# Hedgehog attention and squared-ReLU FFN on one core: q and k crossbar transposes in pieces of four blocks, a PSUM bank kept for zero matmuls, and a new instruction order

## The chip, the cores and the metric

One core of a Trainium2 chip runs the whole program. Times are device microseconds of an execution, given as the median of several runs. A profile is one execution with its own span, the time from the first to the last instruction that the trace holds. The engines are PE (matrix), DVE (vector), ACT (scalar), POOL and SP; SP and POOL here mainly issue DMAs.

## What is computed

```
q, k, v: [8 batches, 8 heads, 576 tokens, 64] f32;  w_phi [64, 128];  w_in [512, 2048];  w_out [2048, 512]
phi(x)  = concat(exp(p), exp(-p)),  p = x @ w_phi - max|x @ w_phi|
kv      = sum over tokens of phi(k) v^T;   z = sum over tokens of phi(k)
attn    = (phi(q) @ kv) / (phi(q) @ z + 1e-6)
x       = attn, heads side by side: [4608 tokens, 512]
out     = max(x @ w_in, 0)^2 @ w_out       [4608, 512] f32
```

Matmul operands are bf16.

## The kernel before

**Work.** Attention runs batch by batch (eight batches of 576 tokens = 512 + 64). The FFN runs in nine chunks of 512 tokens: chunk b takes the first 512 tokens of batch b, and the last chunk takes the eight remainders of 64 tokens. Attention of batch c + 1, the first FFN matmul of chunk c and the second one of chunk c - 1 are mixed, so that PE always has long FFN matmuls beside attention's short ones.

**A batch of attention.** POOL loads k, q and v and casts them to bf16 on the way (`load`, L512 and L520; `load_q`, L532). A batch's k or q lies in SBUF as 18 blocks of 128 x 128, two heads side by side: four groups of four blocks, and a "single" group of two blocks with the 64 last tokens of each head. The blocks have to be transposed. For batches 0 and 1 (`PE_IN`) PE does it (`pe_transposes`, L616), four blocks into one PSUM bank, and DVE or ACT copies them out (L439, L441). For batches 2 to 7 SP issues a crossbar DMA, one for all 18 blocks of k and one for all 18 of q (`transposed`, L626). Then, group by group:

- k: projection (PE, L670 in batch 0, L642 later), largest magnitude per token (DVE, L677, L722), two exponentials (ACT, L705, L728), the scale of v by exp of the maximum (ACT L740 and L747, then DVE L762 and L766), and the sum over tokens (PE, L783 and L788, called KV below), copied to SBUF by ACT or DVE.
- q: projection for the maximum (PE L642 or L816, DVE L823) and, transposed, for the features (PE L858, two exponentials on ACT, L873). The output of eight heads is a matmul with the positive features (PE L888, called NA), a scale of its sum in PSUM (DVE L900), a matmul with the negative ones (L888, NB), a reciprocal (DVE L908) and a product (DVE L912) into `xo`. `xo` is transposed for the FFN: in batch 0 by PE (L928) with copies by DVE (L937), later by a crossbar DMA from SP (L950, four blocks each).

Projections use 64 rows of the array, two side by side; the planner calls them "tiled". All other matmuls use 128 rows.

**FFN.** x times w_in is L1049 in chunk 0 and L1038 later; the ReLU is on ACT (L1015) or DVE (L1017), the square on DVE (L1024); times w_out is L1103 (L1067 for the last quarter); the result leaves PSUM by ACT or DVE (L441, L439) and HBM stores are issued by SP (L1121, L1118, L1090).

**What sets the order.** The program is not issued in the order of the source. Each step is an `Op` with an engine, a cost, a key and its reads and writes. `Machine.run` (a planner that runs while the program is built) replays the engines, the eight PSUM banks and two DMA queues with these costs, and at each step takes the ready Op with the smallest key. Thousands of keys (`KEYS`), release times of loads (`RELEASES`) and a string of bits (`STATES`), which says for each copy and ReLU whether ACT or DVE does it, are written out in the file; `LIM` caps how many PSUM groups of a kind may be open; `SLACK` is what the plan adds to the landing of a DMA. Each engine then issues its instructions strictly in the planned order, and a semaphore wait at the head of a queue holds all that stands behind it. POOL has at most eight DMAs under way: the ninth waits for the first.

**Zero matmuls.** After the plan is made, gaps in PE's planned time before `WARM_UP` = 45 us are filled with matmuls of a zero tile (L1195, `warm`), as many as fit into the planned gap. They write to a PSUM bank that is free at that moment (`op.spare`); where no bank is free, nothing is filled in.

Of the kernel before, what the change touches and what calls it, by code (L numbers as in the profile page):

```python
# [21 lines left out]
SLACK = {"first": 1.2, "v0": 2.5, "ld": 0.8, "x": 1.2, "kq": 1.0}  # L22
# [3 lines left out]
WARM_UP, COLD = 45.0, 6.0  # L26
# [87 lines left out]
class Machine:  # L114
# [7 lines left out]
    def __init__(self, plan, limits, ahead, patience, want):  # L122
        self.plan, self.limits = plan, limits
        self.ahead, self.patience, self.want = ahead, patience, want
        self.free_at = [0.0] * self.BANKS
        self.holding = None
        self.open = {}
        self.q = {"SP": [], "POOL": []}
        self.q_t, self.q_v = 0.0, 0
        self.hist = {"SP": [], "POOL": []}  # L130
# [64 lines left out]
    def run(self):  # L195
# [81 lines left out]
        while left:  # L277
# [19 lines left out]
            spare = next((b for b in range(self.BANKS) if self.free_at[b] <= e["free"] + 1e-9), None) if name == "PE" else None  # L297
            op = pick(name, e, t)
# [31 lines left out]
            if op.closes is not None:  # L330
                g = op.closes
# [19 lines left out]
def kernel(  # L351
# [32 lines left out]
    def pin(ins):  # L384
        i = ins.ins
        before = last_on.get(i.engine)
        if before is not None:
            dep(i, before, mybir.DependencyClass.NoSync)
        last_on[i.engine] = i.name
        if now[0].gate is not None:  # L390
            dep(i, now[0].gate.ins, mybir.DependencyClass.Sync)
        now[0].ins = i.name
        return ins
# [203 lines left out]
    def attention(b):  # L597
        s2 = b % 2
        pe_in = b in K['PE_IN']
# [24 lines left out]
        def transposed(x, xt, tag, ttag, key):  # L624
            def fn():
                pin(nc.sync.dma_start_transpose(out=xt, in_=x))  # L626
            add("SP", (2.8 if tag == "xk" else 3.4, 0), key, fn, r=of(tag, b, (0, 1, "s") if tag == "xq" else (0, 1, 2, 3, "s")),
                w=[(ttag, s2, t) for t in range(18)], dma=(3.6, HW_IN, "x", "kq"), what="X" + tag)

        if not pe_in:  # L630
            transposed(xk[s2], kTb, "xk", "kT", KA(b) - 10)
            transposed(xq[s2], qTb, "xq", "qT", KA(b) - 9)
# [345 lines left out]
        else:  # L978
            if pe_in:
# [235 lines left out]
    'PE_IN': [0, 1],  # L1215
    'PX': [1, 1, 1, 1, 1],
# [5 lines left out]
    'LIM': {'b0': 7, 'att': 3, 'kv': 7, 'op': 6},  # L1222
    'AHEAD': 356.131,
    'PATIENCE': 60.701,
# [4 lines left out]
    '1000000100001001111000110100100000000100010000001001000000010101000010000010001000010010000010000000'  # L1229
    '0100000101001010001110100010101001001000100010011001000101001001101010010100101101100010010100011100'  # L1230
    '0111010111100111100110100000111'
# [3 lines left out]
    17407, 102, 303, -19, 23448, 164, 25399, 7284, 103, -334, -342, 962, 612, -4448, -358, -466, 854, -5120, 1043,  # L1235
    1445, 2531, 2378, 1835, 1683, 1283, 2296, 2776, 6225, 1578, 6847, 9430, 23446, 3002, 6973, 2986, 4636, 7251,
    4704, 6911, 3336, 1003, 977, 1014, 1256, 2044, 19225, 3264, 1208, 2649, 9653, 3031, 2018, 7283, 1699, 1392,
    2415, 2482, 2569, 1938, 7416, 2230, 19677, 19665, 21149, 985, 631, 1829, 1167, 502, 1106, 30444, 1429, 24788,
    11688, 1068, 2741, 2271, 1691, 557, 1483, 638, 1830, 1651, 599, -401, 1899, 768, 1607, 1345, 1946, 17315, 1356,
    23984, 24358, 2102, 2748, 1812, 1047, 7206, 3044, 7208, 17205, 16309, 2884, 1937, 2580, 2117, 23465, 1319,  # L1240
    32941, 353, 6936, 22713, 1482, 1252, 12153, 9984, 23851, 1776, 1870, 28693, 2989, 3338, 9168, 2470, 2176, -1818,
    1746, -2214, 2184, 2431, 2073, 16742, 12309, 3675, 32055, 2751, 2607, 33525, 19924, 2061, 1353, 18117, 879, 666,
    2992, 2848, 2951, 3261, 32406, -843, 2706, 724, 5383, 2189, 3713, -1132, 3059, 22482, 2647, 33607, 2425, 2903,
    3153, 7467, 2946, 17043, 887, 30937, 1975, 19418, 5174, 20405, 3839, 537, 22061, 13862, 4153, 4372, 3313, 3702,
    2934, 2946, 2343, 3093, 22612, 3559, 8512, 2725, 3616, 26332, 29011, 3758, 20842, 6383, 2667, 4917, 3013, 11902,
    5345, 5238, 5921, 9912, 17625, 6541, 2315, 4379, 3435, 538, 4929, 3936, -2259, 3063, 3410, 4141, 23913, 13791,
    14506, 9834, 3978, 4002, 4288, 4215, 2945, 1909, 5362, 5104, 5553, 5287, 3268, 17046, 798, 3707, 2741, -1094,
    3553, 8533, 6784, 7264, 5884, 4403, 7199, 11290, 5958, 4782, 5787, 5872, 5644, 5916, 5299, 5137, 5079, 5080,
    20856, -473, 6391, 5749, 5537, 5046, 6063, 19035, 3357, 9582, 5994, 4922, 5968, 6119, 4977, 6670, 6244, 6483,
    6290, 6698, 19067, 4958, -996, 5517, 5252, 5391, 6788, 5266, 4299, 5039, 2805, 10740, 5284, 7476, 6917, 6887,  # L1250
    9690, 7248, 39413, 1751, 9675, 6437, 28262, 6319, 5577, 6334, 6287, 6302, 18429, 7382, 2955, 6913, 5198, 24236,
    28571, 6767, 6251, 7494, -758, 7560, 8050, 9450, 7621, 8371, 7966, 3353, 2499, 2619, 1952, 6194, 29465, 774,
    5220, 3223, 3756, 4311, 3208, 4062, 4051, 4788, 3955, 479, 4014, 3767, 3800, 3168, 4377, -1024, 4889, 5051,
    4450, 2778, 4515, 7272, 9663, 4340, 4251, 5804, 5006, 4304, 9662, 4907, 2794, 5997, 5050, 5175, 5451, 4923,
    28317, 7970, 4699, 4303, 1709, 9057, 5944, 5392, 4331, 14380, 2713, 4765, 4953, 12329, 4480, 5767, 4592, 6860,
    7810, 10905, 2818, 6137, 4180, 2215, 3286, 7321, 5283, 5241, 5956, 5275, 31537, 7305, 7279, 8169, 7954, 8774,
    7928, 7946, 7447, 7197, 8571, 8788, 8754, 9914, 9151, 8623, 10205, 28753, 9236, 8038, 8574, 22052, 8380, 8450,
    7529, 3291, -2, 11359, 9824, 9084, 13735, 9213, 10106, 8801, 8580, 8548, 9717, 12195, 21514, 9841, 10195, 9372,
    20619, 10629, 7364, 7402, 8587, 6358, 6839, 7541, 9500, 9718, 10799, 10955, 10544, 5683, 2374, 9755, 9159,
    27351, 9417, 9862, 9302, 20470, 32494, 10238, 6138, 7030, 7927, 10849, 9641, 9510, -1016, 20794, 10915, 8427,  # L1260
    -116, 13197, 9447, 9495, 2667, 692, 22484, 20389, 10746, 7094, 9290, 10721, 10810, 18159, 12068, 31380, 28083,
    22915, 1026, -887, 11060, 3635, 11045, 11396, 9857, 12004, 7583, 18462, 8756, 4983, 7513, 8752, 3219, 5133,
    6755, -1, 15253, 5347, 6465, 7754, 11386, 4931, 4785, 5572, 8512, 18443, 10833, 15727, 7521, 27495, 8162, 6150,
    7496, 8751, 8038, 7422, 7940, 3836, 10117, 6091, 22706, 7326, 7703, 13090, 9732, 23399, 8450, 13984, 975, 23532,
    8575, 9687, 9024, 7376, 8938, 10675, 9574, 7478, 8651, 8128, 8849, 5308, 31332, 21114, 8850, 29038, 9584, 6298,
    9555, 13221, 10146, 26486, 9580, 10029, 16988, 7506, 5719, 7874, 7841, 7758, 7389, 9044, 16298, 13239, 12245,
    23349, 9079, 12781, 7480, 11973, 8824, 8823, 6561, 6517, 9711, 10208, 3635, 14886, 9819, 5468, 9796, 10776,
    9740, 9730, 27385, 11031, 18006, 10703, 10132, 14, 10657, 9648, 22562, 10246, 19975, 11130, 25441, 23920, 14604,
    8983, 8228, 15704, 10056, 12998, 9196, -1267, 15126, 10713, -326, 20534, 11321, 11509, 12968, 13034, 11538,
    4820, 11603, 1244, 11706, 11438, 11864, 10659, 15019, 12774, 13092, 11103, 11910, 12865, 11965, 11827, 10973,  # L1270
    -497, 11622, 13807, 31538, 11957, 13552, 5263, 12566, 12058, 10811, 25517, 12045, 9673, -2199, 12689, 6817,
    12468, 25073, 13804, 12710, 12761, 14880, 24784, 5370, 9220, 9204, 17211, 13305, -10, 31398, 22456, 9554, 20134,
    14287, 12831, 14375, 12743, 12421, 8816, 16805, 13198, 13168, 9775, 28439, 11026, 24020, 13360, 3050, 15853,
    1925, -239, 4903, 4986, 16708, 13835, 12965, 12562, 11651, 12912, 24547, -1847, 13009, 10966, -2373, 11087,
    9756, 10945, 10200, 12118, 10502, 10956, 21707, 16803, 17099, 11772, 18442, 13381, 11449, 31507, 22778, 12610,
    11775, 11507, 4434, 11804, 11515, 11801, -528, 11413, 13866, 16900, 5711, 15578, 9473, 13709, 19170, 12569,
    10487, 13433, 22777, 22857, 1833, 12762, 24856, 12485, 11283, 14167, 10087, 13341, 8113, 15210, 20080, 16461,
    14025, 15631, 11608, 14097, 7884, 30686, 20661, 25313, -255, -2159, 24682, 11371, 10070, 11200, 16134, 3932,
# [100 lines left out]
```

## Time and profile before

| what | value |
|---|---|
| median of 8 runs | 362.9 us (361.88 to 363.99) |
| profiled execution | 362.88 us, of which the span is 360.8 us |
| PE busy | 344.7 us (96%), 3412 instructions |
| DVE busy | 292.6 us (81%), 503 instructions |
| ACT busy | 232.0 us (64%), 434 instructions |
| POOL busy | 112.6 us (31%) |
| zero matmuls (L1195) | 118 |
| first FFN matmul (L1049) | starts at 33.1 us |
| last matmul (L1067) | ends at 356.9 us |

A PE that is busy 96% of the span is not 96% useful: a matmul of 128 x 512 has a record of 379 ns, but in a long run one starts every 216 ns (40 of them take 8.63 us in the chain of work that ended last), zero matmuls count as busy, and so does a matmul at half the clock. The tables below are therefore read by starts, by stage.

### The profile page before, as it was taken

What the parts mean: (1) busy time and instruction counts of PE and PEld (TensorE: products, weight loads), DVE (VectorE), ACT (ScalarE), POOL (GpSimd) and SP (SyncE); (2) the same over time, 40 slices, a digit from 0 to 9 for tenths busy, and PEclk for the clock granted to TensorE, in tenths of its full rate; (3) what the DMA queues carried; (4) which work ended last, traced back from release to release, by engine and by line L of the source; (5) the groups of instructions that cost most, each with busy time, mean ns of one, the idle gap of its engine ahead of it and who ended that gap; (6) DMA issues with size and microseconds to landing.
All of it is one profiled execution on the core that took longest, in us unless ns stands there. A gap on an engine that the chain in (4) does not pass through costs nothing.

```text
span 360.8 us, 8564 instructions
## 1 busy us (share of the span) xinstructions
PE 344.7 (96%) x3412; PEld 198.2 (55%) x3442; DVE 292.6 (81%) x503; ACT 232.0 (64%) x434; POOL 112.6 (31%) x167
## 2 busy tenths in 40 slices
PE   8579999999999999999999999999999999999995
PEld 8378886554555555446544555555455554444444
DVE  4998999789999977899789888999798965686131
ACT  2986899588888783959677847957885340310320
POOL 8626638356635851363405211020000000000000
PEclk9959999999999999999999999999999999999999
DMA  8999999997989999898957774447230031100213
GB/s 94 192 201 140 168 187 127 168 158 101 163 146 131 157 125 182 169 149 115 89 115 93 128 94 107 96 69 122 77 100 2 17 95 45 36 0 2 110 35 89
DMA packets 102631, 39.62 MB, mean 110 GB/s; under 512 B 77248, under 2 KB 98112, under 8 KB 102592
## 3 DMA queue, kind: packets, MB, share of 16 engines
q0 software_dynamic: 51744, 18.36, 47.5%
q1 hardware_dynamic: 50608, 20.55, 26.0%
q8 instruction: 27, 0.44, 0.5%
q10 hardware_dynamic: 240, 0.16, 0.2%
q14 instruction: 12, 0.10, 0.1%
HBM read 36.77 MB, written 9.44 MB: 128 GB/s over the span
## 4 chain that ended last, share of the span: by engine, by line
PE 65%; DVE 7%; ACT 7%; issue 2%; DMA 1%; DVEq 0%; ACTq 0%
PE psum L1103 27%; PE psum L1038 24%; PE psum L888 4%; PE psum L783 3%; DVE mq L823 3%; PE psum L642 3%; ACT kp L728 2%; PE psum L858 2%; DVE va L766 2%; ACT kn L728 2%; DMA xq<-in_q_dram 1%; DVE mk L722 1%; PE psum L1067 1%; DVE h L1024 1%; ACT va L740 1%
## 5 line engine op out<-in xcount | busy, mean ns | idle before, releaser
L1103 PE MATMUL psum<-wout,h 128*128 128x512 bf16 x530 | 127.4, 379 | 2.4 <-issue 1.3
L1038 PE MATMUL psum<-xT,win 128*128 128x512 bf16 x448 | 105.0, 379 | 0.5 <-ACT hr L1015 0.4
L1015 ACT ACTIVATE hr<-psum 128x512 bf16<-128x512 f32 x91 | 53.7, 599 | 49.8 <-PE psum L1038 27.5
L1103 PEld LDWEIGHTS <-h 128*128 128x128 bf16 x560 | 50.6, 98 | 56.9 <-issue 2.7
L1038 PEld LDWEIGHTS <-win 128*128 128x128 bf16 x512 | 47.5, 98 | 53.6 <-issue 1.6
L1024 DVE TENSOR_TENSOR h<-hr 128x512 bf16<-128x512 bf16 x144 | 56.9, 416 | 16.2 <-ACT hr L1015 15.3
L873 ACT ACTIVATE qp<-psum 128x1024 bf16<-128x1024 f32 (+1 forms) x40 | 37.3, 938 | 19.8 <-PE psum L858 17.1
L532 POOL DMA_DIRECT2D xq<-in_q_dram x52 | 37.7, 728 | 39.2 <-ACT hr L1015 9.5
L823 DVE TENSOR_REDUCE mq<-psum 128x8 f32<-128x1024 f32 (+1 forms) x40 | 43.7, 1110 | 4.6 <-PE psum L642 3.7
L1017 DVE TENSOR_SCALAR hr<-psum 128x512 bf16<-128x512 f32 x53 | 36.0, 683 | 9.8 <-PE psum L1038 8.3
L722 DVE TENSOR_REDUCE mk<-psum 128x8 f32<-128x1024 f32 (+1 forms) x35 | 38.1, 1108 | 2.5 <-PE psum L642 1.7
L728 ACT ACTIVATE kp<-psum 128x1024 bf16<-128x1024 f32 (+1 forms) x35 | 32.8, 937 | 10.2 <-DVE mk L722 10.2
L766 DVE TENSOR_TENSOR va<-xv,va 128x1024 bf16<-128x1024 bf16 (+1 forms) x36 | 38.6, 1100 | 0.7 <-ACT va L747 0.4
L873 ACT ACTIVATE qn<-psum 128x1024 bf16<-128x1024 f32 (+1 forms) x40 | 37.4, 941 | 2.0 <-PE psum L888 2.0
L900 DVE TENSOR_TENSOR psum<-psum,en 128x520 f32<-128x520 f32 (+1 forms) x40 | 27.9, 700 | 7.6 <-PE psum L888 6.5
L728 ACT ACTIVATE kn<-psum 128x1024 bf16<-128x1024 f32 (+1 forms) x35 | 32.9, 948 | 0.1
L912 DVE TENSOR_TENSOR xo<-psum,rden 128x512 bf16<-128x512 f32 (+1 forms) x40 | 27.3, 686 | 0.9
L512 POOL DMA_DIRECT2D xv<-in_v_dram x26 | 18.9, 726 | 28.7 <-ACT qp L873 10.5
L512 POOL DMA_DIRECT2D xk<-in_k_dram x28 | 20.2, 724 | 21.5 <-ACT va L747 7.4
L783 PE MATMUL psum<-va,kp 128*128 128x65 bf16 x256 | 21.2, 199 | 0.1
L783 PE MATMUL psum<-va,kn 128*128 128x65 bf16 x256 | 21.0, 198 | 0.1
L441 ACT ACTIVATE ot<-psum 128x512 f32<-128x512 f32 x24 | 14.4, 604 | 9.9 <-PE psum L1103 6.6
(68 smaller groups left out, 408.0 us busy)
## 6 DMA issues: line engine op xcount, KB each, us to landing
out_dram<-ot SPq DMA_DIRECT2D x32, 256.0 KB, 2.6
xk<-in_k_dram POOLq DMA_DIRECT2D x26, 128.0 KB, 4.2
xv<-in_v_dram POOLq DMA_DIRECT2D x24, 128.0 KB, 4.1
xq<-in_q_dram POOLq DMA_DIRECT2D x48, 64.0 KB, 3.7
win<-in_moe_w_in_dram POOLq DMA_DIRECT2D x4, 512.0 KB, 11.4
wout<-in_moe_w_out_dram POOLq DMA_DIRECT2D x4, 512.0 KB, 9.2
xq<-in_q_dram POOLq DMA_DIRECT2D x4, 256.0 KB, 8.5
xv<-in_v_dram POOLq DMA_DIRECT2D x2, 512.0 KB, 9.1
```

Of the source, the lines that this page charges most:

```text
L512: pin(nc.gpsimd.dma_start(out=x[:, a * 512 : z * 512].rearrange("p (h x) -> p h x", x=4 * D), in_=src[b][2 * a : 2 * z, 0:512, :].rearrang ...
L532: pin(nc.gpsimd.dma_start(out=x[:, jj * 1024 + a * 256 : jj * 1024 + z * 256].rearrange("p (h x) -> p h x", x=128), in_=q[b][2 * a : 2 * z ...
L722: pin(nc.vector.tensor_reduce(out=mk_view(g), in_=ps2(pj)[:, :, : n * Fd].rearrange("p e (i f) -> p e i f", f=Fd), axis=AX.X, op=ALU.max, ...
L728: pin(nc.scalar.activation(out=dst[slot][:, :, :n, :].rearrange("p e i f -> p e (i f)"), in_=ps2(pj)[:, :, : n * Fd], func=ACT.Exp, scale= ...
L766: pin(nc.vector.tensor_tensor(out=o[:, :, :D], in0=xv[s2][:, 512 * g0 : 512 * g1].rearrange("p (m d) -> p m d", d=D), in1=o[:, :, D].to_br ...
L783: pin(nc.tensor.matmul(out=o[:, sg, hi, :], lhsT=(kp, kn)[sg][kgroup[pr]][:, j % 2, 2 * hi + j // 2, :], rhs=va[s2][sg_of(sg, pr)][:, 8 * ...
L823: pin(nc.vector.tensor_reduce(out=mqb[:, c, :, :n], in_=ps2(pj)[:, :, : n * Fd].rearrange("p e (i f) -> p e i f", f=Fd), axis=AX.X, op=ALU ...
L873: pin(nc.scalar.activation(out=o, in_=i_, func=ACT.Exp, scale=sgn))
L1015: pin(nc.scalar.activation(out=hr[sl], in_=ps1(g), func=ACT.Relu))
L1024: pin(nc.vector.tensor_tensor(out=dst, in0=i_, in1=i_, op=ALU.mult))
L1038: pin(nc.tensor.matmul(out=o, lhsT=win[mc // 4][:, kc, mc % 4 * P : (mc % 4 + 1) * P], rhs=x, start=(kc == 0), stop=(kc == KC - 1)))
L1103: pin(nc.tensor.matmul(out=ps1(g), lhsT=h2[c % 2][mc // 4][:, mc % 4, tt * P : (tt + 1) * P], rhs=wout[mc // 4][:, mc % 4, :], start=(mc = ...
```

## The change

The planner's input changes, one step of the program changes its form, and the order of all instructions follows.

```
-SLACK = {"first": 1.2, "v0": 2.5, "ld": 0.8, "x": 1.2, "kq": 1.0}
+SLACK = {"first": 0.8, "v0": 1.2, "ld": 1.2, "x": 1.3, "kq": 1.6}
-WARM_UP, COLD = 45.0, 6.0
+WARM_UP, RESERVED, COLD = 45.0, 27.0, 6.0
...
-        self.free_at = [0.0] * self.BANKS
+        self.free_at = [0.0] * (self.BANKS - 1) + [RESERVED]
...
+            if name == "PE" and t < RESERVED:
+                spare = self.BANKS - 1
...
-            def fn():
-                pin(nc.sync.dma_start_transpose(out=xt, in_=x))
-            add("SP", (2.8 if tag == "xk" else 3.4, 0), key, fn, r=of(tag, b, (0, 1, "s") if tag == "xq" else (0, 1, 2, 3, "s")),
-                w=[(ttag, s2, t) for t in range(18)], dma=(3.6, HW_IN, "x", "kq"), what="X" + tag)
+            def piece(a, n, srcs):
+                def fn():
+                    pin(nc.sync.dma_start_transpose(out=xt[:, a : a + n, :], in_=x[:, a * P : (a + n) * P]))
+                add("SP", (1.23, 0), key + a * 0.1, fn, r=of(tag, b, [u for u in srcs if u == "s"]) + [t for t in srcs if t != "s"],
+                    w=[(ttag, s2, t) for t in range(a, a + n)], dma=(0.2 * n, HW_IN, "x", "x"), what="X" + tag)
+            for g in range(4):
+                if tag == "xk":
+                    srcs = [(tag, s2, g)]
+                else:
+                    srcs = [(tag, s2, g // 2, y) for y in range(3)][2 * (g % 2) : 2 * (g % 2) + 2] + [(tag, s2, g // 2)] * (g % 2)
+                piece(4 * g, 4, srcs)
+            piece(16, 2, ["s"])
...
     'PE_IN': [0, 1],
+    'PE_Q': [0, 1],
...
-    'LIM': {'b0': 7, 'att': 3, 'kv': 7, 'op': 6},
-    'AHEAD': 356.131,
-    'PATIENCE': 60.701,
+    'LIM': {'tp': 7, 'b0': 4, 'att': 3, 'kv': 4, 'hp': 6, 'op': 5},
+    'AHEAD': 286.558,
+    'PATIENCE': 47.752,
```

1. The crossbar DMA of 18 blocks becomes five, of 4, 4, 4, 4 and 2 blocks, each of which reads only its own part of k or q.
2. Until the plan's 27 us one of the eight PSUM banks is not given to any Op; zero matmuls may always be written there, so every planned gap of PE up to then is filled.
3. `KEYS`, `RELEASES` and `STATES` are new. On every engine the order differs from end to end; the counts differ as follows.

| instruction | before | after |
|---|---|---|
| zero matmul (PE) | 118 | 215 |
| crossbar DMA of k and q (SP) | 12 | 60 |
| ReLU on DVE / on ACT | 53 / 91 | 66 / 78 |
| KV copy on DVE / on ACT | 9 / 23 | 14 / 18 |
| result copy on DVE / on ACT | 11 / 24 | 8 / 27 |
| copy of transposed q, four blocks, on DVE / on ACT | 4 / 4 | 6 / 2 |
| copy of transposed k, two blocks, on DVE / on ACT | 2 / 0 | 1 / 1 |

All other instructions are the same in number and shape. Line numbers of the changed file are 13 higher from the projections on (L1038 becomes L1051).

At the start, POOL's first loads were a single group of v, then k, q, k; they become k, k, a single group of k, q. PE's first Op after the zero matmuls is in both the transpose of four blocks of k, with 52 zero matmuls ahead of it before and 36 after.

## Prediction

> **What bounds the kernel now.** I read the page's 40 slices first, then busy times by stage up to the first FFN matmul, then PE's timeline from start to start, then the waits. All sums are made against the profiled execution: 362.88 us, span 360.8, so 2.1 us lie around the span. It agrees with the median of 362.9.
>
> ```profile
> PE   8579999999999999999999999999999999999995
> ...
> DVE  4998999789999977899789888999798965686131
> ACT  2986899588888783959677847957885340310320
> ...
> PEclk9959999999999999999999999999999999999999
> ```
>
> From the fourth slice (27 us) to the end PE has no slice under nine tenths, while DVE rests in some slices and ACT in most. Only slices two and three show a PE that is not full, and the third has its clock at half. So there is a start, in which something else sets the pace, and a steady part of 320 us that PE sets. By stage (columns: window, length, then busy time and count of PE, weight loads, DVE, ACT, POOL, then the granted clock, DMA share, GB/s):
>
> ```profile
> 6.20:13.00 6.80, 6.28 (x98) 4.81 (x96) 5.12 (x9) 5.21 (x12) 5.72 (x8) 1.00 1.54 185
> 13.00:16.40 3.40, 1.10 (x21) 0.69 (x19) 3.39 (x7) 3.40 (x9) 1.99 (x3) 1.00 1.44 194
> 16.40:21.30 4.90, 1.41 (x12) 1.08 (x12) 4.90 (x11) 4.90 (x16) 2.13 (x3) 0.50 1.33 203
> 21.30:26.60 5.30, 5.23 (x74) 4.99 (x74) 5.00 (x8) 4.16 (x12) 1.33 (x2) 0.50 1.39 197
> 26.60:33.10 6.50, 6.50 (x126) 5.52 (x124) 5.42 (x13) 4.05 (x10) 4.20 (x6) 1.00 1.20 138
> ```
>
> From 13.0 to 21.3 us DVE (8.29 of 8.30) and ACT (8.30 of 8.30) are full and PE is busy for 2.5: PE waits for them. After a stretch with PE at 1.10 of 3.40 the clock is half until 26.6. From 21.3 PE is full, but at half clock: three KV groups take 1.10 us each (starts 23.35, 24.45, 25.55, 26.64), the fourth, at full clock, 0.6. At 33.1 the first FFN matmul starts, and PE is never without work again.
>
> The steady part as a sum: a long run starts a 128 x 512 matmul every 0.216 us. Counting every instruction after 33.1 by such steps (0.031 a KV or NA matmul, 0.028 a projection, 0.057 a short FFN matmul) gives 306.8 us of useful work. What else is in it is seen here:
>
> ```profile
> 84.23 1.46 PE L1038 MATMUL psum<-xT,win 128*128 128x512 bf16 x6
> 85.62 0.39 PE L858 MATMUL psum<-qT,wphi 64*128 64x512 bf16 x2
> 85.85 0.39 PE L642 MATMUL psum<-wphi,kT 64*128 64x128 bf16 x8
> 86.17 0.61 PE L1038 MATMUL psum<-xT,win 128*128 128x512 bf16 x2
> ```
>
> Six long matmuls from 84.23 are due at 85.53, the next starts at 86.17; 0.64 us for contents of 0.23 + 0.22 (8 x 0.028). About 0.2 us is lost by changing to 64-row matmuls and back. The same sum over all 49 such stretches gives a median of 0.21 and 12.3 us in total; plain gaps add 4.2. So 33.1 + 306.8 + 12.3 + 4.2 = 356.4, PE's end (356.9), and 3.9 us of copies and stores to the span's end. Three things can move the time: when the FFN starts, the number of stretches, and new or vanished gaps.
>
> **The change, part by part.**
>
> *First FFN matmul.* It needs the second copy of transposed xo, the end of a DVE chain, and DVE is what was full. Its list up to that copy, by steps from start to start (maxima of k 8 x 0.61 + 2 x 0.40, of q 4 x 1.13 + 0.6, scale of v 10 x 0.61, copies, scales, products), is 23.1 us before: from 6.8 to 32.9, so 3.0 idle. After it is 23.6 (one KV copy and one scale more, fewer transposed-k copies). DVE starts when PE's first transposes end, and they wait for `ident`, which stands behind six POOL DMAs (the last row is PE's):
>
> ```profile
> 5.73 0.35 POOL L1128 TENSOR_SCALAR_AFFINE_SELECT ident<-ident 128x128 bf16<-128x128 bf16 x1
> ```
> ```profile
> 6.36 0.39 PE L616 MATMUL psum<-ident,xk 128*128 128x128 bf16 x4
> ```
>
> After, five DMAs stand ahead (0.71 + 0.78 + 0.66 + 0.92 + 0.66 from 1.25, by the same rows), so `ident` is done at 5.3, the first transposes run at 5.5, and DVE starts 0.9 earlier, at 5.9. Of the 3.0 us idle, 1.0 stood before the scale at 28.40, behind the KV groups at half clock; with full clock it can go. 1.1 stood between 7.2 and 10.3; k now comes first, and its second load is POOL's second, not its fourth, so I take half of it as gone. Idle left: 1.4. Copies end at 5.9 + 23.6 + 1.4 = 30.9, and the FFN starts 0.2 later, at 31.1: **-2.0 us**. Bounds: PE's own list up to there (zero matmuls included, at full clock from 6.2 us, first transposes at 5.5) takes until 29.8, so -3.3 at most; with all 3.0 us of idle time kept it starts at 32.7, -0.4.
>
> *The zero matmuls* cost PE nothing where they fill waits; 97 more of 0.056 are 5.4 us, in a start where PE stood idle for 5.8 us from 13.0 to 21.3. That the clock holds is their gain: three KV groups at 0.6 instead of 1.10 are 1.5 us, but DVE ended its last scale of v at 24.5 and the fourth KV group cannot be earlier; this gain is inside the 2.0, not beside it. The Trainium skill, "TensorE: Matmul & The Clock Gate", section "Why this matters for your kernels", says that the clock drops after a gap of some 3 us without matmuls. The trace disagrees: PE's longest wait between 13.0 and 16.4 was 1.3 us, and the clock was half from 16.4. By the page there was nothing to fill, the 1.0 us ahead of 28.40 would stay, and the sum would be 362.8; by the row the filling is needed, and it is 361.8.
>
> *The bank* is held only until the plan's 27 us, when seven banks must feed DVE and ACT. They were full with eight. If one bank less starves DVE, that is inside the bound of -0.4.
>
> *Crossbar DMAs in pieces.* Rows of both sizes (columns: from issue to landing, us):
>
> ```profile
> xT<-xo SPq DMA_TRANSPOSE x28, 2.5
> ...
> qT<-xq SPq DMA_TRANSPOSE x6, 5.3
> kT<-xk SPq DMA_TRANSPOSE x6, 6.7
> ```
>
> SP was occupied for some 3.1 us by 18 blocks and for 1.2 by four (median of L950). Five pieces are 6.0, so 12 x 2.9 = 35 us more on SP, which issues for some 93 us in all (12 x 3.1, 35 x 1.2, 14 of stores): there is room, though each `xT` transpose and store behind a piece waits up to 1.2 us a piece. The first four blocks land 2.5 us after their load, not 5.3 to 6.7. PE's table of waits holds no wait for a crossbar DMA of q or k, so nothing is saved directly: **0**; bounds -0.5 to +0.5 by SP's order.
>
> *Stretches.* In the order after there are 56 after the first FFN matmul instead of 49. Seven times 0.21 is **+1.5 us**; by the cheapest and dearest common ones (0.10 and 0.43), +0.7 to +3.0.
>
> *Gaps.* Of the 4.2 us in plain gaps and the rest in dear stretches, 1.1 stood between 58 and 66 us around transposes of batch 1's q; there the chain of work runs through a load:
>
> ```profile
> 61.10 4.76 DMA xq<-in_q_dram
> ```
>
> That load is POOL's 55th DMA before and its 38th after, so I take half of the 1.1 as gone: **-0.6**, bounds -1.1 and 0.
>
> *DVE* gets 13 ReLUs (0.68), five KV copies (0.42) and two q copies, and gives three result copies away: +9 us, ACT as much less. Up to the fourth product of batch 4 its list is 157 us before (ended at 182.5, 17.4 idle on the way) and 169 after. PE reaches that chunk's first FFN matmul, at 188.8 before, 1.3 later by its list (+3.3 of earlier work, -2.0). With `xo` 4.2 us ahead of the FFN, as in chunks 5 to 7 before, DVE may idle for 190.1 - 4.2 - 5.9 - 169 = 11 us. Idle time on an engine that was not the bound shrinks by itself, so I put **0** here and its failure among the rivals.
>
> *Tail.* Both orders end with 16 short matmuls, copies and stores: 0.
>
> Sum: -2.0 + 1.5 - 0.6 = -1.1; 362.88 - 1.1 = **361.8 us**.
>
> **The rivals.**
>
> - *The start gains more, and the pieces free SP.* FFN at 29.8 (-3.3), gaps -1.1, +1.5: -2.9, about **359.9**. For it: DVE and ACT were full from 13 to 26 and a smooth order can keep them so. Against it: DVE's list allows 29.5 only with no wait at all.
> - *No change: DVE takes the start's gain back, or the clock drops all the same* (zero matmuls fill the planned gaps, and real ones may lie elsewhere). The FFN starts at 32, -1.1, +1.5, -0.4: **362.9**.
> - *Slower: DVE becomes the bound between 100 and 190 us.* Place: products of batches 2 to 4 and the ReLUs between. If DVE idles more than 11 us up to batch 4's fourth product, PE waits one for one. With the old 17.4 it would be 6.4 us late; half of that is 3.2: 361.8 + 3.2 = **365.0**. For it: DVE was busy 93% from 33 to 111 us and must be 94% on average to 180. Against it: from 13 to 21 it was 100%.
>
> **How the numbers follow.** Forecast (360.6 to 363.0) 0.45; the first rival 0.16; no change 0.18; slower by DVE 0.21. A measurement of this kernel tells 0.3%, 1.1 us, from no change: faster is below 361.8, slower above 364.0. Two thirds of the forecast's cases and the first rival are faster: 0.30 + 0.16 = 0.46. A third of the forecast's and two thirds of the no-change cases are within: 0.15 + 0.12 = 0.27; the rest, 0.06 + 0.21 = 0.27, is slower. The range leaves out a fifth: from a start at PE's bound with gaps gone and cheap stretches (-3.3 - 1.1 + 0.9 = -3.5, 359.4) to half the DVE loss less a little (364.6). The likeliest case's own range is 360.6 to 363.0.
>
> **What would show it.** The clock at 1.00 from 6 to 30 us and four KV groups of 0.6; the first FFN matmul at 31.1; DVE still full from 13 to 26; 56 stretches of 0.21; no load of q on the chain near 60 us; PE with no gap over 0.5 us for a DVE result between 100 and 190. Wrong if the clock drops again, if PE waits for `xo`, or if POOL's load of batch 2 that now stands ahead of batch 0's second piece of k holds that piece back beyond 18 us, where PE's list needs it.

## The result: 366.3 us, slower, and outside the range

The changed kernel takes 366.3 us (364.20 to 369.05, 11 runs) against 362.9 (361.69 to 364.44, 32 runs): 1.0097 times before, 95% interval 1.0077 to 1.0116. The forecast was 361.8, the range 359.4 to 364.6. Its profiled execution took 364.88 us with a span of 363.1, so it lies 1.4 us under its own median. The times of after are spread over 4.9 us, those of before over 2.8.

### The profile after

The slices first, as for before:

```profile
PE   7999999999999999999999999999999999999995
...
DVE  5999999899989999999879987998898962764720
ACT  3986988688777676765688786578585512301311
...
PEclk9999999999999999999999999999999999999998
```

The slice at half clock is gone, and PE is full from the second slice. By these lines alone the change looks like a gain. By stage (columns as before: window, length, busy time and count of PE, weight loads, DVE, ACT, POOL, clock, DMA share, GB/s):

```profile
6.20:13.00 6.80, 6.30 (x102) 4.86 (x100) 5.68 (x11) 5.70 (x15) 4.92 (x7) 1.00 1.41 158
13.00:16.40 3.40, 3.40 (x51) 2.56 (x50) 3.29 (x7) 3.37 (x9) 2.10 (x3) 1.00 1.54 187
16.40:21.30 4.90, 4.60 (x75) 3.89 (x72) 4.81 (x9) 4.75 (x13) 3.51 (x5) 1.00 1.36 202
21.30:26.60 5.30, 5.09 (x103) 4.04 (x103) 5.02 (x7) 4.13 (x11) 3.25 (x5) 1.00 1.38 198
26.60:33.10 6.50, 6.39 (x126) 5.65 (x124) 6.00 (x16) 5.36 (x10) 2.83 (x5) 1.00 1.52 194
```

The clock is 1.00 throughout; PE is busy for 3.40 of 3.40 us where it was for 1.10. But DVE and ACT are as full as they were, and they set the start. The identity is ready 0.7 us earlier (5.37, before 6.08), and the first transposes run 0.9 us earlier (5.43, before 6.36):

```profile
5.02 0.35 POOL L1141 TENSOR_SCALAR_AFFINE_SELECT ident<-ident 128x128 bf16<-128x128 bf16 x1
```
```profile
5.43 0.59 PE L619 MATMUL psum<-ident,xk 128*128 128x128 bf16 x4 [0.41 <-POOL ident L1141]
```

Of that, 0.6 us arrive: the first FFN matmul starts at 32.56 instead of 33.15. DVE's copies that it needs end at 32.45. From DVE's first instruction at 6.05 to there are 26.4 us, 1.6 of them idle, so the list takes 24.8. The same count for before gives 23.8 (6.78 to 32.91, 2.3 idle). One scale of the sum (0.6 us) now stands between the two copies:

```profile
31.36 0.28 DVE L950 COPY xT<-psum 128x256 bf16<-128x256 bf16 x1
31.56 0.70 DVE L913 TENSOR_TENSOR psum<-psum,en 128x520 f32<-128x520 f32 x1
32.17 0.28 DVE L950 COPY xT<-psum 128x256 bf16<-128x256 bf16 x1
```

The load of q that stood on the chain near 61 us is gone from it (the chain of work that ended last, 61 to 62 us; columns: start, length, what):

```profile
60.65 0.49 PE psum L796 x16
61.14 0.11 PE psum L801 x2
61.25 0.11 PE psum L619 x2
61.36 0.49 PE psum L796 x16
```

The loss is in the steady part. The median stretch still costs 0.2 us, but a few of the 56 are much longer. The two longest, in PE's timeline:

```profile
123.13 1.26 PE L1051 MATMUL psum<-xT,win 128*128 128x512 bf16 x5
124.32 0.29 PE L655 MATMUL psum<-wphi,qT 64*128 64x128 bf16 x4
125.25 0.39 PE L871 MATMUL psum<-qT,wphi 64*128 64x512 bf16 x2 [0.64 <-DMA qT<-xq]
...
191.48 0.39 PE L871 MATMUL psum<-qT,wphi 64*128 64x512 bf16 x2
192.43 0.82 PE L1051 MATMUL psum<-xT,win 128*128 128x512 bf16 x3 [0.56 <-DMA xT<-xo]
```

PE waits for a piece of q, and later for a transpose of xo. In before PE's table of waits has no crossbar DMA at all. The rows of crossbar DMAs (last column: us from issue to landing, median):

```profile
kT<-xk SPq DMA_TRANSPOSE x30, 4.5
qT<-xq SPq DMA_TRANSPOSE x30, 4.4
xT<-xo SPq DMA_TRANSPOSE x28, 2.6
```

A piece of four blocks lands after 4.4 us, hardly earlier than the whole of q did (5.3); the trace has single cases from 2.4 to 9.5.

The page of before shows something that the prediction's sums of stretches overlooked (busy us, mean ns, then idle time):

```profile
L1103 PE MATMUL psum<-wout,h 128*128 128x512 bf16 x530 | 127.4, 379 | 2.4 <-issue 1.3
L1103 PEld LDWEIGHTS <-h 128*128 128x128 bf16 x560 | 50.6, 98 | 56.9 <-issue 2.7
```

560 weight loads, but 530 matmuls: 30 matmuls have no record (36 in the changed kernel), and in each of the two profiles 8 of them are the first behind a stretch. There they look like 0.216 us more of the stretch, 1.7 us in all. So the 12.3 us for before become 10.7, and the "dearest common" price of 0.43 is the usual 0.21 with one such matmul behind it. Here and below each of them is put in at its weight load's time.

The account of the span, otherwise made like the prediction's, in us:

| term | predicted | profiled execution |
|---|---|---|
| first FFN matmul | -2.0 | -0.6 (33.15 to 32.56) |
| stretches | +1.5 | +4.7 (10.7 to 15.4) |
| plain gaps over 0.1 us after the first FFN matmul | -0.6 | -1.9 (4.3 to 2.4) |
| sum | -1.1 | +2.2 (span: 360.8 to 363.1, +2.3) |

### The profile page after: what moved, and what is told of

The parts are those of the page before. It is cut to its first block, busy times and chain, and to the rows that moved or that the text cites. A ratio compares the mean times of both kernels' runs of the same rounds, so it can differ in the third digit from the quotient of the medians.

```text
span 363.1 us, 8855 instructions
## 1 busy us (share of the span) xinstructions
PE 350.7 (97%) x3503; PEld 200.2 (55%) x3539; DVE 300.0 (83%) x519; ACT 225.4 (62%) x418; POOL 112.5 (31%) x167
## 4 chain that ended last, share of the span: by engine, by line
PE 66%; ACT 12%; DVE 9%; DMA 7%; issue 4%; POOL 1%; SPq 1%; POOLq 0%; ACTq 0%; DVEq 0%
PE psum L1116 27%; PE psum L1051 22%; PE psum L901 5%; PE psum L655 3%; ACT kp L741 3%; ACT kn L741 2%; DMA xk<-in_k_dram 2%; PE psum L796 2%; DMA xT<-xo 2%; DVE va L779 2%; DVE h L1037 2%; ACT hr L1028 2%; PE psum L871 2%; DMA qT<-xq 1%; DVE mk L735 1%
## 5 line engine op out<-in xcount | busy, mean ns | idle before, releaser
L1116 PE MATMUL psum<-wout,h 128*128 128x512 bf16 x524 | 129.4, 379 | 3.1 <-issue 1.3
L1051 PE MATMUL psum<-xT,win 128*128 128x512 bf16 x448 | 105.4, 379 | 0.6 <-DMA xT<-xo 0.6
L1051 PEld LDWEIGHTS <-win 128*128 128x128 bf16 x512 | 47.2, 98 | 54.4 <-issue 2.6
L1028 ACT ACTIVATE hr<-psum 128x512 bf16<-128x512 f32 x78 | 45.8, 601 | 41.7 <-PE psum L1051 26.8
L1030 DVE TENSOR_SCALAR hr<-psum 128x512 bf16<-128x512 f32 x66 | 44.5, 681 | 7.3 <-PE psum L1051 7.0
L443 ACT ACTIVATE ot<-psum 128x512 f32<-128x512 f32 x27 | 16.1, 596 | 41.7 <-PE psum L1116 39.7
L741 ACT ACTIVATE kn<-psum 128x1024 bf16<-128x1024 f32 (+1 forms) x35 | 32.5, 936 | 0.1
L796 PE MATMUL psum<-va,kp 128*128 128x65 bf16 x256 | 19.8, 194 | 0.3 <-ACT hr L1028 0.3
L796 PE MATMUL psum<-va,kn 128*128 128x65 bf16 x256 | 19.8, 193 | 0.0
```

The costliest lines, as they stand in the source:

```text
L741: pin(nc.scalar.activation(out=dst[slot][:, :, :n, :].rearrange("p e i f -> p e (i f)"), in_=ps2(pj)[:, :, : n * Fd], func=ACT.Exp, scale= ...
L796: pin(nc.tensor.matmul(out=o[:, sg, hi, :], lhsT=(kp, kn)[sg][kgroup[pr]][:, j % 2, 2 * hi + j // 2, :], rhs=va[s2][sg_of(sg, pr)][:, 8 * ...
L1028: pin(nc.scalar.activation(out=hr[sl], in_=ps1(g), func=ACT.Relu))
L1030: pin(nc.vector.tensor_scalar(out=hr[sl], in0=ps1(g), scalar1=0.0, scalar2=None, op0=ALU.max))
L1051: pin(nc.tensor.matmul(out=o, lhsT=win[mc // 4][:, kc, mc % 4 * P : (mc % 4 + 1) * P], rhs=x, start=(kc == 0), stop=(kc == KC - 1)))
L1116: pin(nc.tensor.matmul(out=ps1(g), lhsT=h2[c % 2][mc // 4][:, mc % 4, tt * P : (tt + 1) * P], rhs=wout[mc // 4][:, mc % 4, :], start=(mc = ...
```

## The experiments

Three theories were open. **Transposes**: the new order uses pieces of q and k soon after their issue, and they land late. **SP time**: a piece occupies SP for 1.2 us, and what stands behind it is issued late. **Order**: the new order is longer by itself, by its stretches and its small gain at the start. All ratios are to before, run on the same chip.

### The changed kernel again

No edit.

> The changed kernel unchanged, for a second profile and a second set of times beside the next two: 366.3 (1.0097 of before). All theories alike. The two longest waits of its first profile (1.02 us at 124 us for a crossbar DMA of q, 1.25 us at 190 us for one of xo) are there again if they come from the order, and move if they come from DMAs that share the queue by chance.

365.29 us, 1.0067 (1.0048 to 1.0086). PE waits again at 124 us for a piece of q (1.29 us for that stretch instead of 1.02), and the stretch at 192 us, which ends with a transpose of xo, is long again (0.89). So these places come from the order, and the sizes vary. A third is new: at 176 us (0.81, in the first profile 0.32) PE waits 0.54 us for DVE. In this execution the first FFN matmul starts at 33.4, after a wait of 1.3 us for the first load of q. Over the nine profiles taken with the new order's start and all its zero matmuls it lies between 32.0 and 33.4 (mean 32.5), over the five with the start of before between 32.3 and 33.6 (mean 33.0). So the start's gain is about half a microsecond, less than what it varies by.

### Without the transposes of q and k

```
-                    pin(nc.sync.dma_start_transpose(out=xt[:, a : a + n, :], in_=x[:, a * P : (a + n) * P]))
+                    pass
```

and the same in before.

> The kernel before without its 12 crossbar DMAs of k and q: batches 2 to 7 compute with the transposed k and q of batches 0 and 1. Base line for the next run. All theories: PE waits for none of these transposes, so 362 to 363; if xT transposes and loads gain from the free queue, 361.5.

> The changed kernel without its 60 crossbar DMAs of k and q; batches 2 to 7 compute with the transposed k and q of batches 0 and 1. Theory A: the long waits inside 64-row stretches at 46, 102 and 124 us go, and the one of 1.25 us at 190 us (a transpose of xo that landed 5.0 us after its issue) shrinks since fewer DMAs share the queue: 2 to 3 us less than 366.3, so 363.3 to 364.3, which is what stretches (+1.5) and start (-0.6) leave of the difference. Theory C: under 0.5 us less, 365.8 or more.

Before: 361.69, 0.9984 (0.9969 to 0.9999). Changed: 363.50, 1.0032 (1.0021 to 1.0044), and the 11 runs lie within 1.0 us of each other. The wait at 124 us is gone, the stretch at 190 us shrinks from 1.25 to 0.62; those at 46 us (0.86) and 102 us (0.62) stay. So the transposes carry a part, and the spread, but 363.50 - 361.69 = 1.8 us are the order's own.

### Pieces, or SP's time, in the order of before

```
-                pin(nc.sync.dma_start_transpose(out=xt, in_=x))
+                for a, n in ((0, 4), (4, 4), (8, 4), (12, 4), (16, 2)):
+                    pin(nc.sync.dma_start_transpose(out=xt[:, a : a + n, :], in_=x[:, a * P : (a + n) * P]))
```

> The kernel before, in its own order, with each of its 12 crossbar DMAs of k and q issued as five (4, 4, 4, 4 and 2 blocks) one behind the other. Theory A (the time went to transposes that land later than the new order counts on): splitting by itself costs little, since before's order has long pauses between a whole transpose and its use; SP is occupied 6.0 instead of 3.1 us each time, so a store or an xT transpose behind it is up to 2.9 us later: 362.9 to 364.0. Theory B (pieces cost by themselves, by 48 more DMAs on SP and by DMA share): 365 to 366.5. Theory C (the new order's stretches and its small gain at the start are the whole cause, transposes innocent): 362.9.

376.78 us, 1.0392 (1.0357 to 1.0427): 14 us slower, four times the loss of the whole change. Expected were 363 to 366.5. SP's timeline (columns: start, length, engine, line, operation, tiles, count):

```profile
138.56 7.11 SPq L627 DMA_TRANSPOSE kT<-xk  x5
145.77 6.49 SPq L627 DMA_TRANSPOSE qT<-xq  x5
152.35 1.22 SPq L951 DMA_TRANSPOSE xT<-xo  x1
153.67 6.48 SPq L627 DMA_TRANSPOSE qT<-xq  x5
160.24 0.53 SPq L1122 DMA_DIRECT2D out_dram<-ot  x1
160.86 1.25 SPq L951 DMA_TRANSPOSE xT<-xo  x1
```

SP has no pause for 25 us. In before the same three whole transposes took 10.4 us (4.34 + 3.29 + 2.76), and here 20.1. PE's waits show who stood behind them:

```profile
PE psum L1039 <- DMA xT<-xo: 5.1, 5, 1.7
PE psum L643 <- DMA qT<-xq: 4.4, 2, 2.3
```

To tell SP's time from the transfers, whole transposes were kept and SP was occupied behind them:

```
                 pin(nc.sync.dma_start_transpose(out=xt, in_=x))
+                for _ in range(5):
+                    pin(nc.sync.dma_start(out=scr[0:1, 16 * count_[0] : 16 * count_[0] + 16], in_=ident[0:1, 0:16]))
+                    count_[0] += 1
...
```

> The kernel before with its 12 whole crossbar DMAs, and behind each of them on SP five DMAs of 32 bytes from SBUF to SBUF: SP is occupied for some 2.7 to 3 us more each time (0.53 us a plain DMA in the trace), as with pieces, and next to nothing more is moved. Theory SP time (pieces cost because each occupies SP for 1.2 us, and what stands behind them is issued late): about as long as before with pieces, 372 to 378 us. Theory transfers (pieces cost because small transposes land late beside loads): 363 to 364.

378.13 us, 1.0399 (1.0359 to 1.0439), as long as with pieces. In the order of before it is SP's time that makes pieces dear. A part of the 14 us is the clock's: after such waits it is at half again, from 159.8 to 166.7 and from 170.1 to 173.5 us with pieces, and with SP occupied for 3.4 us in each of two places.

### SP's time in the new order

```
-                    pin(nc.sync.dma_start_transpose(out=xt[:, a : a + n, :], in_=x[:, a * P : (a + n) * P]))
+                    for src in (ident, ident):
+                        pin(nc.sync.dma_start(out=scr[0:1, 16 * count_[0] : 16 * count_[0] + 16], in_=src[0:1, 0:16]))
+                        count_[0] += 1
```

> The changed kernel in which each of the 60 crossbar DMAs of k and q is replaced by two DMAs of 32 bytes from SBUF to SBUF that wait for nothing: SP is occupied as long (2 x 0.6 us against 1.2 to 1.3), the transposes are left out, and batches 2 to 7 compute with the transposed k and q of batches 0 and 1. Theory SP time: the transposes of xo between them are issued as late as in the changed kernel, the wait at 190 us stays near 0.9 to 1.2 us, and of the 2 to 2.8 us that leaving everything out saves about half stays: 364.3 to 365.3. Theory transfers: as with everything left out, 363.5.

The second run has the piece of k or q in place of the first `ident`.

> As the run before, but the first of each two small DMAs reads from the piece of k or q, so that SP also waits there until POOL's load has landed, as the transposes do; the transposes are left out. Theory head of line (what stands behind a transpose on SP waits for that transpose's load): 0.5 us or more above the run before, 365 to 366. Theory SP time alone: equal to the run before. Theory transfers: 363.5.

364.04 us, 1.0039 (1.0016 to 1.0061), and 364.26, 1.0036 (1.0017 to 1.0054). Without any of this occupation it was 1.0032. The intervals overlap. The medians lie 0.5 to 0.8 us apart, but before itself took 0.5 us longer on the chip of these two runs (362.98 against 362.45). The stretch at 190 us stays at 0.90 in the first, as the theory of SP time said, and is 0.61 in the second, so one execution does not decide it. In the new order SP's time and its waits for loads are at most a small part of the loss. That fits a plan that counts 1.23 us of SP for each piece, which the old one did not; no run shows that this is the reason. The theory of SP time holds for pieces put into the old order, and explains little in the changed kernel.

### Plain copies for transposes

```
-                    pin(nc.sync.dma_start_transpose(out=xt[:, a : a + n, :], in_=x[:, a * P : (a + n) * P]))
+                    pin(nc.sync.dma_start(out=xt[:, a : a + n, :], in_=x[:, a * P : (a + n) * P].rearrange("p (t x) -> p t x", t=n)))
+                    small()
```

and likewise for xo; `small` is one DMA of 32 bytes.

> The changed kernel with every crossbar DMA (60 of k and q, 35 of xo) made a plain copy of the same bytes from SBUF to SBUF, with one DMA of 32 bytes behind it so that SP is occupied as long (2 x 0.6 us); the transposition itself is left out, so the operands of PE are in the wrong layout. Loads, waits for loads, order and PE's waits for the copies stay. Theory landing (crossbar transposes land late beside loads, 5.2 instead of 2.4 us): plain copies land in 2 to 3 us, the waits at 124 and 190 us go, 363.3 to 364.3. Theory late issue (loads and SP run 2 to 3 us behind the plan, and whatever is issued then comes too late): copies of the same bytes come as late, waits of 0.5 us or more stay there, 365 to 366.3.

> Control: the kernel before with its 47 crossbar DMAs made plain copies of the same bytes, with DMAs of 32 bytes behind them (four behind 18 blocks, one behind four) so that SP is occupied as long; the transposition is left out. PE waited for none of them but a few of xo, so 361.7 to 362.9 by all theories; 362.9 or more if SP's time is longer than meant.

Changed: 363.98 us, 1.0043 (1.0030 to 1.0055), all runs within 0.9 us. Before: 362.61, 1.0003 (0.9991 to 1.0015). Loads, order and waits are those of the changed kernel, and SP issues the piece of q at the same time (120.09, before the edit 119.97); but PE does not wait for it, and the stretch at 190 us is 0.60:

```profile
124.15 0.28 PE L662 MATMUL psum<-wphi,qT 64*128 64x128 bf16 x4
124.30 0.39 PE L878 MATMUL psum<-qT,wphi 64*128 64x512 bf16 x2
```

DMA rows from 108 to 130 us, first of the changed kernel (packets, MB and share of a queue; then us to landing), then with plain copies:

```profile
q1 hardware_dynamic: 5672, 2.05, 41.6%
...
xT<-xo SPq DMA_TRANSPOSE x3, 2.4
qT<-xq SPq DMA_TRANSPOSE x3, 4.9
```
```profile
q1 hardware_dynamic: 2574, 2.03, 29.5%
...
xT<-xo SPq DMA_DIRECT2D x3, 128.0 KB, 2.0
...
qT<-xq SPq DMA_DIRECT2D x3, 128.0 KB, 3.5
```

The same bytes take less than half the packets (the queue's stores are the same in both). The copies of q land 1.4 us earlier (3.5 against 4.9), those of xo 0.4 earlier (2.0 against 2.4). Over the whole span pieces of k and q land after 4.5 and 4.4 us, plain copies of four blocks after 3.1 and 3.0, and POOL's loads of k in 4.2 instead of 4.8. The Trainium skill, "Advanced Engine Details and Errata", section "X-Bar Transpose (TRN2)", says that transpose DMAs are as fast as regular ones. These rows differ, by 0.4 to 1.5 us. The number of loads in flight alone does not set the difference: the two late transposes of q were issued beside three and four loads, but one of xo that was issued at 109.92 beside five landed after 2.40.

The theory of transposes holds for the wait at 124 us, which is the end of a chain: a load of q issued at 115.62 lands at 119.90, SP issues its transposes at 119.97 and 121.35, they land at 125.21 and 126.26, and PE was ready at 124.6. Whether tying the load to an earlier instruction would have been enough was not tried.

### Zero matmuls

```
-            while op.spare is not None and idle + ...
+            while not 12.0 < op.at < RESERVED and op.spare is not None and idle + ...
```

> The changed kernel without the 110 zero matmuls ahead of steps planned between 12 and 27 us; the bank is still kept. If they hold the clock: it is half again from about 16 to 27 us, the KV groups take 1.1 instead of 0.6 us, the first FFN matmul starts at 33.0 to 34.0 instead of 32.5, and the time is 0.5 to 1.5 us longer (366.8 to 367.8). If the real matmuls of the new order hold it without them: clock 1.00, no change. If the zero matmuls stand in the way of real ones: first FFN matmul at 32.0 and 0.5 us less.

368.27 us, 1.0169 (1.0142 to 1.0196), 0.7 to 1.0% longer than the changed kernel. Two stages of its profile:

```profile
13.00:16.40 3.40, 2.02 (x14) 1.01 (x13) 3.40 (x7) 3.40 (x8) 2.11 (x3) 0.82 1.52 188
16.40:21.30 4.90, 3.33 (x23) 2.13 (x24) 4.52 (x9) 4.55 (x13) 3.51 (x5) 0.50 1.38 199
```

The clock falls to half at 15.2 us. In the 3.41 us ahead of that PE is busy for 1.79 and waits at most 0.71 at a time; its longest wait from 11 to 28 us, 1.42, comes later. So the zero matmuls hold the clock. How the half clock costs 2.6 us or more is not shown: in this execution, which took 366.54, the first FFN matmul starts at 33.25, 0.7 later than in the changed kernel's profile but within the 32.0 to 33.4 of the nine, and PE waits 1.3 us for a result copy of ACT near 124 us.

In the order of before no bank is free for them, so they were put into unused halves of banks:

```
+HALVES = [(15.0, 15.2, 4, 384), (16.9, 17.0, 2, 0), (18.4, 18.5, 6, 384), (21.6, 21.8, 4, 384)]
...
-                pin(nc.tensor.matmul(out=psum[:, op.spare, :P], lhsT=warm, rhs=warm, start=True, stop=True))
+                pin(nc.tensor.matmul(out=psum[:, bank, c0 : c0 + P], lhsT=warm, rhs=warm, start=True, stop=True))
```

> The kernel before in its own order, with 108 zero matmuls more in PE's planned gaps between 13.9 and 21.7 us, written to the unused halves of PSUM banks that hold transposes or a two-block projection, so that no bank is taken from the plan. If it is lack of matmuls that halves the clock in before: clock 1.00 from 13 to 27 us, KV groups of 0.6, the idle 1.0 us of DVE ahead of 28.40 goes, first FFN matmul at 32.0 to 32.6, total 0.5 to 1.1 less than before (361.4 to 362.0). If the zero matmuls stand in the way of real ones: first FFN matmul at 33.1 or later, 363.

365.09 us, 1.0070 (1.0045 to 1.0094), slower than before:

```profile
19.91 0.61 PE L617 MATMUL psum<-ident,xq 128*128 128x128 bf16 x8
22.81 4.30 PE L1202 MATMUL psum<-warm 128*128 128x128 bf16 x45 [2.29 <-ACT qT L442]
27.04 0.39 PE L859 MATMUL psum<-qT,wphi 64*128 64x512 bf16 x1
```

The 45 zero matmuls wait for ACT's copy out of the other half of their bank and then run for 4 us in front of the projection that they were to bridge; the first FFN matmul starts at 37.1. In four of its six executions the clock is at 0.999 or 1.000 throughout, and they take 364.0 to 365.1 us, still more than before (363.27 on this chip). So in the old order these zero matmuls cost more than the clock gives. It shows what the kept bank is for: a zero matmul must have nothing to wait for.

What the clock is worth in the old order can be read from the five profiles with the start of before. Where it is at half for 10.2 us the first FFN matmul starts at 33.15, 33.52 and 33.57; in the two where it is at half for only 6.8 us, at 32.29 and 32.49. So 3.4 us more at half clock go with about 1 us more at the start. Less of it is left at the end: of the 74 executions of before beside these experiments, the 22 with a mean clock of 0.989 or more take 362.4 us on average, the 46 with 0.985 to 0.988 take 362.8.

### SP's queue relieved

Three edits of the changed kernel meant to issue transposes earlier. Stores issued by POOL:

```
-                        pin(nc.sync.dma_start(out=o, in_=ot[sl]))
+                        pin(nc.gpsimd.dma_start(out=o, in_=ot[sl]))
```

> The changed kernel with 32 of its stores (0.53 us of SP each) issued by POOL instead of SP, each at its own place in the order. Theory SP time: the crossbar DMAs behind them are issued up to 0.6 us earlier per store, 364 to 365.5. Theory transfers: the same bytes are moved, 366 to 367. Against both: POOL's loads behind a store wait for its ot; if that decides, 367 or more.

Stores put off on SP behind transposes:

```
+        if op.eng == "SP" and op.what == "st":
+            last = min([at[o] for o in op.succ], default=len(order))
+            j = max([k for k in range(i + 1, last) if order[k].eng == "SP" and order[k].what[0] == "X" and order[k].at < op.at + 5.0], default=i)
...
```

> The changed kernel complete, with one change on SP alone: each store is put behind the crossbar DMAs that the plan has within the next 5 us, as far as nothing that follows it needs it earlier. Stores have a ring of three buffers and are not waited for. Theory SP time: the transposes behind a store are issued 0.6 us earlier for each, PE's waits at 124 us (1.0 to 1.3) and at 176 to 192 us (1.2 to 1.7 in sum) shrink by half, 364 to 365. Theory transfers or chance: 365.3 to 366.3.

And transposes of xo ahead of pieces as well (the same search, for pieces, with 2.7 us).

> As the run before, and in addition pieces of k and q go behind transposes of xo that the plan has within 2.7 us after them, and the 64-token transposes of xo, which only the last chunk reads, are put off like stores. Theory SP time: the wait for a transpose of xo at 190 us goes (it is issued 1.3 us earlier), 0.5 us below the run before, 363.5 to 364.5; still above before by the dearer stretches. If pieces of k or q become late by this instead: waits for qT or kT near 100 to 190 us, 365 or more.

All three came out slower: 367.82 (1.0155, 1.0114 to 1.0196), 379.25 (1.0453, 1.0428 to 1.0478) and 375.62 us (1.0336, 1.0316 to 1.0356). The waits of PE with stores put off:

```profile
PE psum L796 <- ACT ot L443: 5.6, 1, 5.6
PE psum L1051 <- ACT ot L443: 2.6, 1, 2.6
PE psum L1051 <- DVE ot L441: 2.0, 1, 2.0
```

and ACT's, in the same profile:

```profile
ACT ot L443 <- DMA out_dram<-ot: 11.2, 2, 6.5
```

The expectation said that stores are not waited for. They are: a result copy needs one of three buffers, the store that frees it stands behind a transpose that waits for its input, ACT stands at the copy, and PE at whatever ACT does next. The third edit took less but had the same waits (the longest of PE 5.2 us); its clock is at half for 3.4 us in the middle, where that of the second is for 10.2. With POOL's stores PE waits 2.3 us for a copy at 121 us. None of the variants beats before or the changed kernel.

## Why the prediction was wrong

- **The clock and the zero matmuls: right.** Full clock from 6 us, four KV groups of 0.6, DVE full from 13 to 26. The row was the better guide than the rule weighed there: without the zero matmuls the clock halves after no wait over 0.71 us.
- **First FFN matmul: right kind, too large**, -2.0 against -0.6. DVE starts at 6.05 (predicted 5.9) and idles 1.6 us (1.4), but its list takes 24.8 us, where 23.6 were counted. Of the 1.2, 0.7 were missing from the count of before already (23.1, by the count above 23.8), and 0.5 are new: the list got 1.0 longer, not 0.5, and a 0.6 us scale stands just before the last copy. So "copies end at 30.9" failed; they end at 32.45.
- **Stretches: the term that sank the sum**, +1.5 against +4.7, outside its bounds of +0.7 to +3.0. The failed step is "seven times 0.21": a median price for stretches that a new order adds. Without any transposes of q and k the term is still +3.4 (10.7 to 14.1). The stretches under 0.3 us are 45 both times; those over 0.3 rise from 4 to 11 and their sum from 1.9 to 5.1 us, which is nearly all of it. What the dear ones are, the profile of the changed kernel tells: of its 11, two wait for the crossbar DMAs at 124 and 192 us, and in eight a projection starts 0.05 us after the end of an ACT or DVE instruction that reads PSUM. At 55 us, for example, `kn` ends at 54.84 and the projection starts at 54.89:

```profile
53.79 1.05 ACT L741 ACTIVATE kn<-psum 128x1024 bf16<-128x1024 f32 x1
```
```profile
54.89 0.40 PE L655 MATMUL psum<-wphi,qT 64*128 64x128 bf16 x8
```

  So a dear stretch is a short wait for ACT or DVE, mostly too short for the table of waits (0.5 us at 46 and 0.3 at 102 us are in it). That it is a wait for the PSUM bank which they read is likely from the times; no run tested it.
- **Crossbar DMAs, "0; bounds -0.5 to +0.5": failed.** The step took 2.5 us to landing from the row of `xT`; the pieces' own rows are 4.4 and 4.5. It also read from before's waits that "nothing is saved directly", and took that for "nothing is lost": the old order issued whole transposes so early that their time did not matter, the new one does not. Cost in the profiled execution, where the prediction had 0: 0.7 at 124 us (1.02, without the transposes 0.32) and 0.6 at 190 us (1.25 less 0.62) = 1.3, which is the rest of the +4.7. "There is room" on SP, as a mean over the span, was false for the old order (14 us) and true for the new one.
- **Gaps: better than predicted**, -1.9 against -0.6; the load near 61 us left the chain.
- **The slower rival had the sign, not the cause.** DVE was to become the bound from 100 to 190 us; it is 97% busy from 115 to 155 (38.67 of 40 us), but from 100 to 190 us PE waits for a DMA, for ACT and not for DVE; in the second execution it waits once for DVE, 0.54 us at 176. Two of the prediction's signs of being wrong are there, but small or with another cause: PE waits 0.30 us at 19.3 for a load of k, and at 192 us for xo, whose transpose lands late (5.0 us after its issue).

What is shown: of a loss of 2.0 us (second set of times) to 3.4 us (first set), 1.4 to 1.8 us stay when transposes are replaced or left out in both kernels (363.98 - 362.61; 363.50 - 361.69); these are the order's. The rest comes with the transposes of q and k, by their landing, since neither SP's time nor its waits bring it back. How large that rest is varies: 0.2 to 0.6 us of the second set, 1.6 to 2.0 of the first; the intervals of the second set and of the plain copies overlap (1.0048 to 1.0086; 1.0030 to 1.0055).

What stays open: why the median of the first set lies 1.4 us over its own profiled execution. With plain copies, or with nothing in the place of the transposes, the spread is about 1 us; with small DMAs in their place single runs reach 367.0 and 368.3, so it is not their landing alone. Which waits grow in the longer runs was not seen. Their mean clock says that half clock is a part in some: it is 0.994 and 0.995 in the two longest of the first set (368.08 and 369.05), but 0.997 to 1.000 in the others, one of 367.33 among them.

## What to carry to other kernels

The time from issue to landing of a DMA has to be taken from rows of the same kind of transfer with the same traffic beside it. A step that nobody waits for in the old order is free only as long as the new order keeps its lead; ask what lead the new order leaves. And when each stretch of an order costs something, count the dear ones, because the median says nothing about what seven more of them will be. Where a profile has more weight loads than matmuls, put the missing matmuls in before gaps are priced.

## What was not expected of the hardware

- A crossbar transpose of four blocks occupies SP for 1.2 us, 18 blocks for about 3.1; five pieces in place of one made the old order 14 us slower.
- The same bytes moved as crossbar transposes take 5672 packets against 2574, and from 108 to 130 us those of q land after 4.9 against 3.5 us; over the span it is 4.4 against 3.0.
- The clock halves after 3.41 us in which PE was busy for 1.79 and never waited longer than 0.71.
- With one and the same order the clock at the start is at half for 10.2 us in some executions and for 6.8 in others, and the first FFN matmul moves by about 1 us with it.
- Zero matmuls into one half of a PSUM bank waited 2.29 us for a copy out of the other half. The program set that wait; whether the chip needs it was not tried.
